# Issue order of the attention weights at the start of a four-block kernel

## The chip, the cores and the metric

The kernel runs on one core of one Trainium2 chip. The metric is device time in microseconds, the median over runs of the whole program. A lower number is better. One further execution was taken with the hardware profiler; its span runs from the first to the last instruction.

## The reference

The program applies four residual blocks to `x` (2048 tokens of width 512, bf16): A, B, A, B, each after a layer norm. Block A is a recurrent attention with a memory of 8 rows: it goes through 64 segments of 32 tokens in order, and the memory rows of one segment's output are the memory of the next. Block B is a linear attention over all tokens at once. Both A blocks use the same weights.

```python
for s in range(n_seg):                       # 64 segments of 32 tokens
    xs = x[:, s * seg_len:(s + 1) * seg_len, :].copy()
    h = jnp.concatenate([mem, xs], axis=1)   # 8 memory rows, 32 tokens
    q = jnp.einsum('btd,dhe->bhte', h, Wq)   # Wq, Wk, Wv: 512 x 32 heads x 128
    k = jnp.einsum('btd,dhe->bhte', h, Wk)
    v = jnp.einsum('btd,dhe->bhte', h, Wv)
    scores = jnp.einsum('bhqe,bhke->bhqk', q, k) * scale
    scores = jnp.where(mask[None, None], scores, -1000000000.0)
    p = _softmax(scores, axis=-1)
    o = jnp.einsum('bhqk,bhke->bhqe', p, v)
    o = jnp.einsum('bhte,hed->btd', o, Wo)   # Wo: 32 heads x 128 x 512
    mem = o[:, :M, :].copy()
    outs.append(o[:, M:, :])

x = x + _A_ref(_layernorm(x, axis=-1), A_mem0, A_Wq, A_Wk, A_Wv, A_Wo, A_seg_len)
x = x + _B_ref(_layernorm(x, axis=-1), B_wqkv, B_wo)
x = x + _A_ref(_layernorm(x, axis=-1), A_mem0, A_Wq, A_Wk, A_Wv, A_Wo, A_seg_len)
x = x + _B_ref(_layernorm(x, axis=-1), B_wqkv, B_wo)
```

## The kernel before

**Weights.** `Wq_sb`, `Wk_sb`, `Wv_sb` and `Wo_sb` hold the four weights of block A in SBUF, 4 MB each, for the whole program. The first three are loaded by one DMA each from ACT's queue (line 651). `Wo_sb` comes in four quarters of 1 MB from SP's queue (line 656). Quarters 0 and 1 carry a dependence on the key load (`late[1]`), quarters 2 and 3 on the value load (`late[2]`). The load of block B's `wqkv` follows on SP (line 658) and depends on the last quarter in program order; POOL's load of block B's output weight (line 663) depends on that one.

**A segment.** `a_layer` goes over the 64 segments. Memory rows and the first 24 tokens of a segment make one block of 32 columns; the last 8 tokens of four segments together make another, the left block of a group of four segments (`left_block`). For each block, `project` (matmul line 785) multiplies with a weight into one PSUM bank, 16 matmuls for one of two halves of the heads, four of them side by side in column tiles. `turned` copies the result to an image in SBUF and transposes it, either on PE (line 807, evacuated through line 619 or 618) or, for later left blocks and some keys, with a DMA transpose from SP's queue (line 798). Images of left blocks take turns in two slots; an image is not overwritten before the DMA transpose that reads it has landed. Then come the scores of the memory rows (line 876), their sums and values (lines 903, 916, 917), the scores within the left block (line 835), attention of the tokens (lines 948, 945, 971, 972), the output projection with `Wo_sb` (line 999), and with line 1024 the memory rows for the next segment. Line 618 is the evacuation of a PSUM bank when ACT does it, line 619 when DVE does it. A few matmuls on unused data (line 735, `warm`) stand in the first segment.

In the first segment the transposes from SP's queue are those of the left block of the second group, which the planner brings forward into the head of the program: four of them, called T1 to T4 here in their order on SP. Line 835 for that group needs all four.

**Order of the work.** The order on every engine is made before the program is emitted. Each operation is added to a list with its engine or engines, a cost, and what it reads and writes. `schedule` then walks a modelled time. Whenever an engine is free it takes, among the operations whose inputs are ready in the model, the one with the highest priority. For an operation with a place the priority is minus its due time, which is its step times `PERIOD` plus an entry of the table `OFFSET`:

```python
        for nd in nodes:
            nd.prio = nd.tail
            if nd.key is not None and OFFSET:
                step, name, k = nd.key
                nd.prio = -(step * PERIOD + OFFSET[name][k])
```

Operations without a place, such as the four quarters of `Wo`, have as priority the length of the longest modelled chain of work behind them. `finalize` turns dependences into semaphore waits: an instruction waits on its engine's in-order queue, and all that stands behind it waits too. PSUM banks are given out in the course of the same planning.

**The loads at the start.** They carry places with large negative steps:

```python
    P.at(-9000, "ld0")
    P.at(-8000, "ld1")
    for i, (W, v, nm, t) in enumerate(((Wq_sb, qk_view[0], "Wq", 13.2), (Wk_sb, qk_view[1], "Wk", 23.7),
                                       (Wv_sb, qk_view[2], "Wv", 34.8))):
        P.at(-9000 + 1000 * i, "ld%d" % (2 + i))
```

`ld0` is the load of the first memory, `ld1` that of the first 128 rows of `x`, both on SP; `ld2`, `ld3` and `ld4` are the loads of Wq, Wk and Wv on ACT. The step of Wv is -7000, but its offset of -27049.20 puts its due time ahead of the others, so ACT issues Wv, Wq, Wk. The last numbers (13.2, 23.7, 34.8) are the modelled landing times, used only for planning.

Of the kernel before, what the change touches and what calls it, by code (L numbers as in the profile page):

```python
# [22 lines left out]

PERIOD = 13.5
OFFSET = {
    "ld0": (-123.05,),
    "ld1": (-42.20,),
    "ld2": (6.75,),
    "ld3": (-61.40,),
    "ld4": (-27049.20,),  # L30
    "startF": (31.55,),
    "prepF": (60.65, -70.40, -52.45, 13.25, -87.60, -51.75, -71.05, 30.70, -58.30, 4.70, -58.20),
    "left0F": (-67.40, -16.05, 42.40, -9.10, 43.45, -14.00, -72.75, 13.95, -5.65, 15.60, -9.65, -120.75, 45.95,
# [1303 lines left out]
```

## Time and profile before

| | |
|---|---|
| median of 3 runs | 1804.88 us (1804.27 to 1810.15) |
| profiled execution | 1801.99 us |
| its span | 1799.8 us, mean granted TensorE clock 0.991 |
| PE busy | 1690.6 us (94%) |
| PE weight loads | 1138.5 us (63%) |
| ACT busy | 1166.0 us (65%) |
| DVE busy | 954.5 us (53%) |
| POOL busy | 325.9 us (18%) |
| PE's first matmul with Wq | 24.43 us after the start of the span |
| PE's first matmul with Wk | 35.94 us |
| PE's first matmuls with Wv | from 49.88 us |
| PE's first matmul with Wo | about 61.1 us |

The busy shares are averages over the span; the head of the program, before the first matmul with `Wo_sb`, is about 61 of the 1800 us and has its own limits. PE is the tensor engine's matmuls and PEld its weight loads, which overlap. SPq and ACTq are the queues of DMA issues on those engines. An idle time labelled "issue" is one for which the profile shows no wait. Rows of one line and shape are merged in the timeline, so a row's length can span pieces of other rows.

### The profile page before, as it was taken

To read this page: it belongs to the slowest core of one execution; us is meant where nothing else is said; L and a number is where in the kernel's file an instruction comes from. 1 tells how busy PE (TensorE), PEld (TensorE's weight loads), DVE (VectorE), ACT (ScalarE), POOL (GpSimd) and SP (SyncE) were. 2 spreads that over 40 slices of the span, in tenths; PEclk is the share of its full clock that TensorE was granted. 3 is DMA by queue.
4 is the path that set the end of the run, shared out by engine and by line. 5 is a ranking of instruction groups with operands and counts; after the bars stand their busy time and mean duration, and the time that the engine had idled before them with its cause. 6 is when DMAs were issued, how large, how long until landed. Compare 5 with 4: busy or idle time off the path is not lost.

```text
span 1799.8 us, 104863 instructions
## 1 busy us (share of the span) xinstructions
PE 1690.6 (94%) x48407; PEld 1138.5 (63%) x48407; DVE 954.5 (53%) x3216; ACT 1166.0 (65%) x3109; POOL 325.9 (18%) x660
## 2 busy tenths in 40 slices
PE   3899999999999999999889999999999999999997
PEld 1566676667666676676556666666666666666673
DVE  2355455555555555555554555555555555545456
ACT  2566666666666666666556666666667677666665
POOL 2012111211211121121101112222111222211220
PEclk9999999999999999999999999999999999999998
DMA  8412222222222222122111222212222222231223
GB/s 341 116 38 41 45 44 47 42 47 42 45 43 42 47 44 45 41 44 46 28 24 33 48 46 45 50 44 45 47 44 51 44 45 48 47 47 40 57 65 110
DMA packets 235080, 99.29 MB, mean 55 GB/s; under 512 B 213624, under 2 KB 228784, under 8 KB 233104
## 3 DMA queue, kind: packets, MB, share of 16 engines
q1 hardware_dynamic: 211312, 60.22, 17.1%
q0 software_dynamic: 21744, 19.78, 4.7%
q10 hardware_dynamic: 1584, 12.58, 1.7%
q8 instruction: 379, 6.21, 1.4%
q14 instruction: 61, 0.50, 0.1%
HBM read 29.63 MB, written 10.49 MB: 22 GB/s over the span
## 4 chain that ended last, share of the span: by engine, by line
PE 75%; DMA 12%; DVE 5%; ACT 3%; issue 2%; POOL 1%; ACTq 0%; DVEq 0%
PE pb L785 38%; PE pb L999 13%; DMA arena_sb<-arena_sb 9%; PE pb L971 3%; PE pb L1161 3%; PE pb L876 3%; PE pb L807 2%; PE pb L903 2%; DMA Wk_sb<-in_A_Wk_dram 2%; PE pb L1195 2%; POOL dx_sb L634 1%; ACT arena_sb L618 1%; DVE arena_sb L619 1%; PE pb L948 1%; PE pb L1024 1%
## 5 line engine op out<-in xcount | busy, mean ns | idle before, releaser
L618 ACT ACTIVATE arena_sb<-pb 128x512 bf16<-128x512 f32 (+5 forms) x1387 | 705.5, 511 | 330.6 <-PE pb L785 275.7
L634 POOL DMA_DIRECT2D dx_sb<-y_sb x504 | 253.2, 509 | 869.5 <-DVE y_sb L1035 491.8
L785 PE MATMUL pb<-Wv_sb,arena_sb 128*32 128x512 bf16 x5120 | 380.2, 380 | 0.0
L619 DVE COPY arena_sb<-pb 128x512 bf16<-128x512 bf16 (+2 forms) x365 | 131.5, 361 | 398.0 <-PE pb L807 382.5
L785 PE MATMUL pb<-Wq_sb,arena_sb 128*32 128x512 bf16 x5120 | 320.7, 381 | 10.2 <-DMA Wq_sb<-in_A_Wq_dram 9.9
L999 PE MATMUL pb<-Wo_sb,arena_sb 128*32 128x256 bf16 x10368 | 317.2, 274 | 7.5 <-DVE arena_sb L920 7.3
L785 PE MATMUL pb<-Wk_sb,arena_sb 128*32 128x512 bf16 x5120 | 320.2, 381 | 3.8 <-DMA Wk_sb<-in_A_Wk_dram 3.3
L999 PEld LDWEIGHTS pb<-Wo_sb,arena_sb 128*32 128x32 bf16 x10368 | 264.5, 97 | 30.7 <-DVE arena_sb L920 17.7
L785 PEld LDWEIGHTS pb<-Wq_sb,arena_sb 128*32 128x32 bf16 x5120 | 141.8, 97 | 132.1 <-DMA Wq_sb<-in_A_Wq_dram 10.2
L785 PEld LDWEIGHTS pb<-Wk_sb,arena_sb 128*32 128x32 bf16 x5120 | 134.7, 97 | 119.7 <-DVE arena_sb L619 11.1
L619 DVE CAST arena_sb<-pb 128x512 bf16<-128x512 f32 (+3 forms) x346 | 165.0, 478 | 70.4 <-PE pb L785 37.6
L619 DVE COPY arena_sb<-arena_sb 32x320 bf16<-32x320 bf16 (+1 forms) x677 | 150.1, 222 | 81.0 <-PE pb L876 62.7
L618 ACT ACTIVATE outW_sb<-pb 128x128 fp32r<-128x128 f32 x323 | 89.6, 277 | 124.4 <-PE pb L999 118.9
L876 PEld LDWEIGHTS pb<-arena_sb 128*32 128x32 bf16 x8128 | 109.5, 94 | 84.5 <-DMA arena_sb<-arena_sb 35.3
L876 PE MATMUL pb<-arena_sb 128*32 128x8 bf16 x8128 | 131.5, 174 | 29.8 <-DMA arena_sb<-arena_sb 24.5
L785 PEld LDWEIGHTS pb<-Wv_sb,arena_sb 128*32 128x32 bf16 x5120 | 121.8, 95 | 55.1 <-issue 1.6
L971 PE MATMUL pb<-arena_sb 128*128 128x128 bf16 x1024 | 145.3, 218 | 1.4 <-issue 0.6
L887 ACT ACTIVATE arena_sb<-pb 128x192 bf16<-128x192 f32 (+1 forms) x256 | 83.8, 328 | 93.7 <-PE pb L876 92.1
L972 PE MATMUL pb<-arena_sb 128*128 128x32 bf16 x1024 | 127.4, 178 | 0.1
L1035 DVE TENSOR_TENSOR y_sb<-pb,outW_sb 64x256 bf16<-64x256 f32 x158 | 65.9, 417 | 97.0 <-ACT outW_sb L618 93.6
L807 PEld LDWEIGHTS pb<-id_sb,arena_sb 128*32 128x32 bf16 x4352 | 84.3, 96 | 44.7 <-issue 8.1
L894 DVE TENSOR_TENSOR arena_sb<-arena_sb 128x128 bf16<-128x128 bf16 x504 | 90.1, 221 | 39.6 <-ACT arena_sb L887 38.7
(116 smaller groups left out, 2139.8 us busy)
## 6 DMA issues: line engine op xcount, KB each, us to landing
arena_sb<-arena_sb SPq DMA_TRANSPOSE x368, 2.8
Wv_sb<-in_A_Wv_dram ACTq DMA_DIRECT2D x1, 4096.0 KB, 13.6
Wq_sb<-in_A_Wq_dram ACTq DMA_DIRECT2D x1, 4096.0 KB, 23.1
Wk_sb<-in_A_Wk_dram ACTq DMA_DIRECT2D x1, 4096.0 KB, 34.1
Wo_sb<-in_A_Wo_dram SPq DMA_DIRECT2D x4, 1024.0 KB, 7.1
xs_scratch<-x_sb POOLq DMA_DIRECT2D x32, 128.0 KB, 2.2
pq_scratch<-arena_sb POOLq DMA_DIRECT2D x32, 128.0 KB, 2.0
dx_sb<-y_sb POOLq DMA_DIRECT2D x252, 12.0 KB, 2.0
```

What stands on the lines that cost most here:

```text
L618: return e.activation(o() if callable(o) else o, i() if callable(i) else i, ACTF.Copy)
L619: return e.tensor_copy(o() if callable(o) else o, i() if callable(i) else i)
L634: add(eng, lambda e: e.dma_start(o, i), 0.55 if eng == "pool" else 0.4, reads=reads, writes=writes, dsem="%s%d" % (kind, k), lat=lat + (0. ...
L785: r = pe.matmul(tl.f32()[32 * j:32 * j + 32, 0:512], blk[:, c, :], W[:, c, o:o + 512], start=(c == 0), stop=(c == 3), tile_position=(0, 32 ...
L807: r = pe.transpose(tt.bf16()[32 * j:32 * j + 32, 128 * i:128 * i + 128], img[:, k, o:o + 32], id_sb[:, :], tile_position=(0, 32 * j))
L876: r = pe.matmul(tl.f32()[32 * j:32 * j + 32, 48 * i + o:48 * i + o + n], kk[:, hh, j, :], qT[:, hh, j, 0:n], start=True, stop=True, tile_p ...
L887: add("act", lambda a: a.activation(PQ[:, r2, b, :, 0:nq], tl.f32()[:, 0:192].rearrange("p (i q) -> p i q", i=4)[:, :, 0:nq], ACTF.Exp, sc ...
L894: add("dve", lambda v, a=a: v.tensor_tensor(Pm[:, k, a, :].rearrange("p (i j x) -> p i j x", i=4, j=4), PQ[:, r2, b, :, 40 * a:40 * a + 8] ...
L971: pe.matmul(o, vimg[:, r2, e], Pbx[:, hh, :, 0:32], start=True, stop=False)
L972: return pe.matmul(o[:, :, 24:32], vleft[:, g2, e], Pbx[:, hh, :, 32:40], start=False, stop=True)
L999: r = pe.matmul(tl.f32()[32 * j:32 * j + 32, 0:256], oT[:, 4 * hh + n, :], Wo_sb[:, 8 * n + hh, 256 * d:256 * d + 256], start=(hh == 0 and ...
L1035: add("dve", lambda v: v.tensor_tensor(y_sb[0:64, k, :], tl.f32()[0:64, 0:256], outW[64:128, w, :].bitcast(F32), ALU.add), c_dve(256), rea ...
```

## The change

Five entries of `OFFSET` become zero. With them the due times are -121500 for the first memory and for Wq, -108000 for the first rows of `x` and for Wk, and -94500 for Wv.

```diff
--- before.py
+++ after.py
@@ -23,11 +23,11 @@
 
 PERIOD = 13.5
 OFFSET = {
-    "ld0": (-123.05,),
-    "ld1": (-42.20,),
-    "ld2": (6.75,),
-    "ld3": (-61.40,),
-    "ld4": (-27049.20,),
+    "ld0": (0.00,),
+    "ld1": (0.00,),
+    "ld2": (0.00,),
+    "ld3": (0.00,),
+    "ld4": (0.00,),
     "startF": (31.55,),
     "prepF": (60.65, -70.40, -52.45, 13.25, -87.60, -51.75, -71.05, 30.70, -58.30, 4.70, -58.20),
```

ACT then issues Wq, Wk, Wv. The planner runs again from these due times, so that the order of some work in the first segment moves too. On PE, with shapes as the emitted program has them (- before, + after; "x16" is sixteen matmuls; the rows shown are those around the first key matmuls and the last value matmuls ahead of `Wo`):

```diff
-L785 Matmult pb<-Wq_sb,arena_sb 32x512 x12
+L785 Matmult pb<-Wq_sb,arena_sb 32x512 x16
 L715 Matmult pb<-arena_sb 128x128
 L785 Matmult pb<-Wq_sb,arena_sb 32x512 x4
-L785 Matmult pb<-Wk_sb,arena_sb 32x512 x48
+L785 Matmult pb<-Wk_sb,arena_sb 32x512 x4
+L785 Matmult pb<-Wq_sb,arena_sb 32x512 x4
+L785 Matmult pb<-Wk_sb,arena_sb 32x512 x8
+L785 Matmult pb<-Wq_sb,arena_sb 32x512 x8
+L785 Matmult pb<-Wk_sb,arena_sb 32x512 x36
...
-L785 Matmult pb<-Wq_sb,arena_sb 32x512 x16
...
+L785 Matmult pb<-Wv_sb,arena_sb 32x512 x12
 L971 Matmult pb<-arena_sb 128x128
 L972 Matmult pb<-arena_sb 128x4x8
...
+L785 Matmult pb<-Wv_sb,arena_sb 32x512 x4
 L835 Matmult pb<-arena_sb 32x32 x32
-L785 Matmult pb<-Wv_sb,arena_sb 32x512 x16
 L999 Matmult pb<-Wo_sb,arena_sb 32x256 x64
```

On ACT, the evacuation that waits for the landing of T1 (the second query image of the left block) now stands ahead of the first key images; the evacuation of the mask block goes from ACT to DVE. The order on SP and POOL is the same as before.

## The prediction

> **What bounds the kernel now.** I read the table of DMA issues first, since the edit moves DMA issues. Its columns are destination and source, queue, count, size, and us from issue to landing.
>
> ```profile
> Wv_sb<-in_A_Wv_dram ACTq DMA_DIRECT2D x1, 4096.0 KB, 13.6
> Wq_sb<-in_A_Wq_dram ACTq DMA_DIRECT2D x1, 4096.0 KB, 23.1
> Wk_sb<-in_A_Wk_dram ACTq DMA_DIRECT2D x1, 4096.0 KB, 34.1
> Wo_sb<-in_A_Wo_dram SPq DMA_DIRECT2D x4, 1024.0 KB, 7.1
> ```
>
> Three equal loads go out within 1.5 us and land about 10 us apart, one after another: values, queries, keys. The timeline of the first 64 us (start, length, engine, line, operands, idle time before and its releaser) says who needs them when.
>
> ```profile
> 24.43 4.25 PE L785 MATMUL pb<-Wq_sb,arena_sb 128*32 128x512 bf16 x40 [9.90 <-DMA Wq_sb<-in_A_Wq_dram]
> 33.35 1.30 SPq L798 DMA_TRANSPOSE arena_sb<-arena_sb  x1
> 35.92 1.02 SPq L656 DMA_DIRECT2D Wo_sb<-in_A_Wo_dram  x2
> 35.94 4.05 PE L785 MATMUL pb<-Wk_sb,arena_sb 128*32 128x512 bf16 x48 [3.26 <-DMA Wk_sb<-in_A_Wk_dram]
> ...
> 43.35 5.16 SPq L798 DMA_TRANSPOSE arena_sb<-arena_sb  x2
> 45.85 0.25 PE L835 MATMUL pb<-arena_sb 128*32 128x32 bf16 x11 [2.27 <-issue]
> 48.55 1.21 SPq L656 DMA_DIRECT2D Wo_sb<-in_A_Wo_dram  x2
> ...
> 49.88 0.10 PEld L785 LDWEIGHTS pb<-Wv_sb,arena_sb 128*32 128x32 bf16 x3
> 53.16 1.19 SPq L798 DMA_TRANSPOSE arena_sb<-arena_sb  x1
> 59.10 0.30 PE L835 MATMUL pb<-arena_sb 128*32 128x32 bf16 x16 [1.84 <-DMA arena_sb<-arena_sb]
> 59.22 1.89 PE L785 MATMUL pb<-Wv_sb,arena_sb 128*32 128x512 bf16 x16
> 60.88 2.70 PE L999 MATMUL pb<-Wo_sb,arena_sb 128*32 128x256 bf16 x64
> ```
>
> PE waits 9.90 us for Wq and 3.26 us for Wk, while Wv, landed at 14.4, is first read at 49.88. The chain of waits over the first 90 us agrees: its two long DMA pieces are
>
> ```profile
> 1.83 34.07 DMA Wk_sb<-in_A_Wk_dram
> ...
> 53.16 5.80 DMA arena_sb<-arena_sb
> ```
>
> The second is the fourth transpose, queued behind the last two Wo quarters. From 64.8 us PE runs from segment to segment, and no wait there names a weight load. So the head is DMA-bound, and what it ends earlier the whole kernel ends earlier.
>
> Last, the DMA view of 6 to 8 us, where ACT's loads (q10, 8 KB packets) meet an x load on SP's queue (q1, 1 KB) and POOL's (q0):
>
> ```profile
> q10 hardware_dynamic: 70, 0.57, 69.2%
> q0 software_dynamic: 64, 0.20, 24.7%
> q1 hardware_dynamic: 72, 0.07, 10.3%
> ```
>
> 72 packets against 70: the queues take turns packet by packet, not byte by byte.
>
> **What the Trainium skill says.** "DMA: Bandwidth & Descriptors", Queues, rings and completion order: each engine goes round its queues in turn, and descriptors of one queue are consumed in ring order. The packet counts above agree, and so does the fourth transpose, which needs 5.8 us behind Wo where a free queue takes 2.5. "Runtime: NRT & Kernel Launch", Instruction fetch mechanics: instructions come in 16 KiB blocks over a DMA queue of their own. The trace has such a fetch at 43.26 to 44.34 us, and PE, idle for "issue" since 43.6, goes on at 45.85. "TensorE: Matmul & The Clock Gate", What's actually happening: a free-running window of about 3.4 us decides between half and full clock. Here the clock is half from 35.16 to 38.57 and from 59.05 to 62.47, 3.41 us each, after idle stretches.
>
> **The change, part by part.** Five start offsets become zero. Two of them are no change of order: x and memory inputs stay first on SP. ACT's three issues become Wq, Wk, Wv. SP's order is unchanged: transpose T1; Wo quarters 1 and 0 (waiting for Wk); T2, T3; quarters 3 and 2 (waiting for Wv); T4; wqkv. What is new is when those waits end. Wk lands second, Wv last, so the first two quarters now start while Wv is still moving. On PE the same matmuls are reordered within the first segment; from the second segment on, order and waits are the same on every engine but for a few waits already met, with PSUM banks renamed.
>
> 1. *Queries.* The first load now feeds PE. It lands at 0.80 + 13.6 = 14.4, so PE starts at 14.45 instead of 24.43: 9.98 us gained. Its inputs are ready: the first group's evacuations end by 13.1, the rest at 15.96, when PE is still in its first cold groups (0.43 us for four matmuls, so the first evacuation came 2.8 us after the start).
> 2. *Keys.* Query work took 24.43 to 32.7, so it ends near 22.7. The second load lands at 24.4. The old third one was late by some 1.5 us on one DMA engine (15 of its 16 completions by 34.3, the last at 35.90, after an instruction fetch and T1). Those meet Wk again at the same distance, so I take 25.9: 10.0 us earlier, with the PE idle as long as before.
> 3. *The 2.27 us instruction stall* stays: its fetch again falls among weight traffic. Shifted, PE goes on at 35.9; up to 1 us later if two loads delay the fetch more than one.
> 4. *Values.* Old third landing 34.3 without the fetch. Added: T1 in the middle of the stream, about 1 us (its data took 34.6 to 35.9); Wo's packets one for one with some 370 remaining packets of Wv, 46 against 309 ns, so 7.4 us become 8.5, +1.1; a fetch on one engine, +1.1. That is 37.5. PE asks at 49.88 - 10.0 = 39.9. Hidden, with 2.4 us to spare; without that cover each us is a us.
> 5. *SP's queue, the next thing late.* By Wv's end Wo has moved 370 KB of its first 2048. The rest at the 355 KB/us of 40 to 43 us takes 4.7 us: 41.8. T2 and T3, waiting behind it, 1.1 us each: 44.0. Quarters 3 and 2, 2048 KB at about 345: 50.0. T4: 51.0, landed 51.3. Before, 58.97; so T4 gains only 7.7 of the 10. ACT's evacuation for T4's image waits for T3, which lands near 44.3, not 42.5; the attention work behind it on ACT moves 1.8 us, and PE would reach the L835 pair near 49.7. So T4 still decides.
> 6. *After T4.* Before, PE then ran L835 (0.30), 16 Wv matmuls (1.71, cold) and L999 at 61.11. Now the Wv matmuls stand ahead of L835: L999 starts at 51.3 + 0.14 + 0.30 = 51.75. That is 9.36 us earlier. L999 took 2.5 us with part of it cold; all warm it is 1.77 (the next segment's), all cold 3.5. I charge 0.3.
>
> Sum: 9.36 - 0.3 = 9.1 us. The span goes from 1799.8 to 1790.7, the profiled execution from 1801.99 to 1792.9. The median of the runs, 1804.88, is 2.9 above that execution; taken from it the time is 1795.8.
>
> Moved but free: the mask-block evacuation goes from ACT to DVE, which idles there; wqkv waits for quarter 3 and then T4, lands near 55 instead of 62.9, and is first needed when block B starts, tens of us later.
>
> **Unknowns, bounded.** T1 now flows against a full stream of 8 KB packets; the trace shows it only against the tail of one. If its 32 rows on each engine go as a burst, as T2's and T3's do alone, it costs about 1 us and lands near 26.5 to 28; PE's next query image needs it at 28.5. If each row of 256 bytes takes turns with an 8 KB packet, 32 x 0.33 = 10.6 us, so it lands at 35. I take the burst: POOL's 1 KB packets that meet a transpose later in the trace are held for 1 us and more, not the transpose. Clock: the phase of the half-rate stretches may cost or give 1.7 us. Both ends are kept in the range.
>
> **Rivals.**
>
> *T1 crawls behind Wv.* ACT's in-order queue has the second query image (it waits for T1) ahead of the key images. With T1 landed at 35, ACT stands from about 28 on, PE soon after, and the key images come out at 36.1 to 38.5 instead of 39.2 to 41.8: only 3.3 to 3.6 us are gained, 1801.4. For it: strict turns in the lines above. Against it: the held POOL packets.
>
> *The queue costs less than I say.* If Wo moves faster or T4 slips in early, PE is the limit: it comes to L835 at 47.9, L999 at about 48.8, saving 12: 1793.
>
> *Wv becomes the bound.* The wait only changes its name from Wk to Wv. If the queues shared by bytes, Wv would land near 41, and PE would wait 1 us, still less than T4 costs. It would have to land after 44 to erase more than 3 us; this only widens the forecast.
>
> *Slower.* The renamed PSUM banks stay renamed through all 128 segments. If a clash of banks cost each segment 0.15 us, 19 us would be lost, 10 more than gained: 1814.8. It decides above 0.07 us a segment, and would be measurably slower above 0.115. Nothing in the trace names a bank as a reason for waiting, and every wait is on the same producers as before.
>
> **How the numbers follow.** Likeliest 0.68: 1795.8, own range 1793.3 to 1798.3. Queue faster 0.08: 1793. T1 crawls, or some mixture of late T1, T3 and fetch, 0.17: 1801.4. Banks 0.07: 1814.8. About 0.3%, 5.4 us, is what a measurement here can tell from no change. Faster: 0.68 + 0.08 = 0.76; same 0.17; slower 0.07. Range 1792.5 to 1801.8: it leaves out the bank case, the far edge of the crawl, and a little below.
>
> **What would show it.** Right: PE's first query group near 14.5, key group near 25.9, no wait for Wv, T1 landed before 28.5, T4 near 51 and L999 near 51.8, then the same length to the end as before. Wrong: a long ACT wait for a transpose near 28; PE waiting for Wv; T4 landed after 54; or a span from L999 to the end that grew.

## The result and the profile after

The changed kernel takes 1804.45 us (median of 4 runs, 1802.95 to 1808.35) where the kernel before took 1805.18 us beside it (4 runs, 1804.27 to 1810.15). The ratio is 0.9994, 95% interval 0.9969 to 1.0018: no difference. The forecast was 1795.8 us, and its range ended at 1801.8. A later comparison with more runs (22 against 59) gives 0.998, interval 0.9968 to 0.9992, so 1.4 to 5.8 us of a forecast of 9.

Executions of one kernel spread over 8 to 15 us here (the kernel before: 1801.88 to 1816.36 in those 59). Where a step of 1 to 5 us in the head of the program is in question, I therefore go by the traces, of which there are two for each kernel.

| us from the start of the span | before | before, again | after | after, again | forecast |
|---|---|---|---|---|---|
| PE's first matmul with Wq | 24.43 | 24.28 | 14.45 | 14.57 | 14.45 |
| PE's first matmul with Wk | 35.94 | 35.64 | 25.88 | 25.54 | 25.9 |
| Wv landed | 14.45 | 14.29 | 37.16 | 36.80 | 37.5 |
| T1 landed | 36.38 | 36.54 | 37.37 | 37.00 | 26.5 to 28 |
| T2, T3 landed | 45.87, 49.79 | 45.84, 49.32 | 43.73, 47.48 | 43.39, 47.03 | by 44.0 |
| T4 landed | 58.97 | 58.84 | 56.61 | 56.26 | 51.3 |
| first line-1024 group (end of the head) | 63.96 | 62.25 | 59.34 | 59.12 | none given |
| second line-1024 group (end of segment 1) | 75.13 | 74.24 | 73.62 | 74.08 | none given |
| span | 1799.8 | 1802.2 | 1803.3 | 1802.7 | 1790.7 |

The loads came as foreseen. The table of DMA issues of the changed kernel:

```profile
Wq_sb<-in_A_Wq_dram ACTq DMA_DIRECT2D x1, 4096.0 KB, 13.6
Wk_sb<-in_A_Wk_dram ACTq DMA_DIRECT2D x1, 4096.0 KB, 24.6
Wv_sb<-in_A_Wv_dram ACTq DMA_DIRECT2D x1, 4096.0 KB, 35.3
Wo_sb<-in_A_Wo_dram SPq DMA_DIRECT2D x4, 1024.0 KB, 11.8
```

The three places are taken by Wq, Wk, Wv, about 11 us apart. Wo's quarters now take 11.8 us instead of 7.1, because two of them, issued at 25.85 and 26.29, stand behind T1 in SP's ring: Wo's first packet moved at 33.78. The timeline of the head of the changed kernel (start, length, engine, line, operands, idle time before and its releaser):

```profile
14.45 3.95 PE L785 MATMUL pb<-Wq_sb,arena_sb 128*32 128x512 bf16 x40
22.80 1.33 SPq L798 DMA_TRANSPOSE arena_sb<-arena_sb  x1
25.85 7.18 SPq L656 DMA_DIRECT2D Wo_sb<-in_A_Wo_dram  x2
25.88 0.62 PE L785 MATMUL pb<-Wk_sb,arena_sb 128*32 128x512 bf16 x4 [3.26 <-DMA Wk_sb<-in_A_Wk_dram]
37.46 1.57 ACT L618 ACTIVATE arena_sb<-pb 128x512 bf16<-128x512 f32 x3 [14.68 <-DMA arena_sb<-arena_sb]
38.08 8.11 SPq L798 DMA_TRANSPOSE arena_sb<-arena_sb  x2
38.59 0.62 PE L807 MATMUL pb<-id_sb,arena_sb 128*32 128x128 bf16 x16 [6.59 <-ACT arena_sb L618]
47.93 1.69 PE L785 MATMUL pb<-Wv_sb,arena_sb 128*32 128x512 bf16 x28
51.16 1.19 SPq L798 DMA_TRANSPOSE arena_sb<-arena_sb  x1
56.74 0.28 PE L835 MATMUL pb<-arena_sb 128*32 128x32 bf16 x16 [0.67 <-DMA arena_sb<-arena_sb]
57.03 1.93 PE L999 MATMUL pb<-Wo_sb,arena_sb 128*32 128x256 bf16 x64
```

The 9.90 us of waiting for Wq are gone, and a new wait has come: ACT stands idle for 14.68 us, and a transpose ends it. It is the evacuation of the second query image of the left block, which may not overwrite its slot before T1 has landed. PE had finished its matmuls by 28.6, so nearly 9 us of it are due to T1. Behind it in ACT's queue are the evacuations of the key images, so PE, done with the key matmuls, stands with it, 6.59 us by the profile. The pieces of over 5 us made of transposes in the chain of waits say the same:

```profile
22.80 14.57 DMA arena_sb<-arena_sb
...
51.16 5.44 DMA arena_sb<-arena_sb
...
61.94 5.18 DMA arena_sb<-arena_sb
```

The first is T1 and the second T4. The third is new too: two key transposes of segment 1, which took about 2.9 us in the kernel before (issued 66.56, landed 69.42). The head is 4.62 us shorter than before, and segment 1 gives 3.11 of it back (63.96 to 75.13 took 11.17 us before; 59.34 to 73.62 takes 14.28). In the second pair of traces the head wins 3.13 us, and 2.97 are given back (11.99 us of segment 1 against 14.96).

Last, the DMA view of 29 to 31 us: q10 carries Wv in packets of 8 KB, q1 carries T1 in rows of 256 bytes. The columns are packets, MB, and their share of 16 engines.

```profile
q10 hardware_dynamic: 100, 0.82, 97.7%
q1 hardware_dynamic: 98, 0.03, 5.5%
```

98 rows go against 100 packets: one for one. T1's 512 rows, 32 for each of the 16 engines, start from 26.8 to 36.6 us. In the kernel before they did so from 34.6 to 35.9. Taking turns is not all of these 9.9 us. By 33.5 us 315 rows had moved. Then Wv ran out (23 packets in the half us before, 10 and 2 in the two after), and 109 rows moved in half a us. The last row moved at 36.63, 0.4 us after Wv's last packet (36.24). So T1 kept pace with Wv's packets while these lasted, and landed when the last straggling ones were over.

### The profile page after: what moved, and what is told of

It is laid out like the page before. It is cut to its first block, busy times and chain, and to the rows that moved or that the text cites. A ratio compares the mean times of both kernels' runs of the same rounds, so it can differ in the third digit from the quotient of the medians.

```text
span 1803.3 us, 104862 instructions
## 1 busy us (share of the span) xinstructions
PE 1692.2 (94%) x48407; PEld 1140.7 (63%) x48407; DVE 954.7 (53%) x3217; ACT 1165.2 (65%) x3108; POOL 325.9 (18%) x660
## 4 chain that ended last, share of the span: by engine, by line
PE 73%; DMA 14%; DVE 6%; ACT 3%; issue 2%; POOL 2%; DVEq 0%; SPq 0%; ACTq 0%
PE pb L785 37%; PE pb L999 13%; DMA arena_sb<-arena_sb 12%; PE pb L971 3%; PE pb L1161 3%; PE pb L876 3%; PE pb L807 2%; PE pb L903 2%; POOL dx_sb L634 2%; PE pb L1195 1%; DVE arena_sb L619 1%; DMA dx_sb<-y_sb 1%; ACT arena_sb L618 1%; PE pb L948 1%; PE pb L917 1%
## 5 line engine op out<-in xcount | busy, mean ns | idle before, releaser
L999 PE MATMUL pb<-Wo_sb,arena_sb 128*32 128x256 bf16 x10368 | 316.7, 273 | 7.5 <-DVE arena_sb L920 6.7
L999 PEld LDWEIGHTS pb<-Wo_sb,arena_sb 128*32 128x32 bf16 x10368 | 263.8, 97 | 30.3 <-DVE arena_sb L920 17.3
L785 PEld LDWEIGHTS pb<-Wv_sb,arena_sb 128*32 128x32 bf16 x5120 | 121.5, 95 | 55.3 <-issue 1.0
L807 PE MATMUL pb<-id_sb,arena_sb 128*32 128x128 bf16 x4352 | 109.1, 220 | 7.6 <-ACT arena_sb L618 7.1
## 6 DMA issues: line engine op xcount, KB each, us to landing
Wo_sb<-in_A_Wo_dram SPq DMA_DIRECT2D x4, 1024.0 KB, 11.8
```

Of the source, the lines that this page charges most:

```text
L785: r = pe.matmul(tl.f32()[32 * j:32 * j + 32, 0:512], blk[:, c, :], W[:, c, o:o + 512], start=(c == 0), stop=(c == 3), tile_position=(0, 32 ...
L807: r = pe.transpose(tt.bf16()[32 * j:32 * j + 32, 128 * i:128 * i + 128], img[:, k, o:o + 32], id_sb[:, :], tile_position=(0, 32 * j))
L999: r = pe.matmul(tl.f32()[32 * j:32 * j + 32, 0:256], oT[:, 4 * hh + n, :], Wo_sb[:, 8 * n + hh, 256 * d:256 * d + 256], start=(hh == 0 and ...
```

## The experiments

Two theories were to be told apart at first. **A**: T1 crawls behind Wv, and the evacuation that waits for its slot at the head of ACT's queue takes the gain. **B**: the sheer traffic of Wv and Wo makes everything late. In all diffs below, which are shortened, "-" is the changed kernel. A head or a second group that is some us "ahead" is measured from the first trace of before; from its second trace it is 1.71 us less in the head and 0.89 us less at the second group.

### T1 to T4 from images of their own

```diff
-            nd = evac(img[:, k, :], ...)
+            nd = evac(own_img[n], ...)        # n = 0..3, buffers that are free at this time
```

> The changed kernel, but the four transposes T1 to T4 read images in buffers of their own, so no evacuation waits for a transpose to land; SP's order becomes T1, T2, two Wo quarters, T3, T4, two Wo quarters. Theory A (T1 crawls behind Wv, and ACT's in-order queue stands behind the image slot that T1 holds): T1 still lands near 37 us, but ACT doesn't stand; the first key images come near 28.5 instead of 38, PE has no 6.6 us wait for ACT, the first matmul with Wo moves from 57.0 to 51 to 53, and the first memory step (L1024) from 59.3 to 53 to 55. Theory B (the head is bound by the sheer traffic of Wv and Wo, the wait for the slot only covers it): PE waits for Wv or Wo instead, and Wo starts not before 56.

1801.23 us (one run; before on the same chip 1804.72, median of 23). T1 again crawled (48 rows against 48 packets of 8 KB in each us from 25 to 31, landed at 36.15), and now nothing on ACT waited for it; the key matmuls, transposes and scores ran from 25.7 to 35.7. But with these images the planner put T2 ahead of Wo and T3 and T4 between its quarters, and its PE order asks for them earlier. The timeline:

```profile
46.48 0.48 PE L844 MATMUL pb<-arena_sb 128*32 128x32 bf16 x32 [7.10 <-DMA arena_sb<-arena_sb]
```

PE waited 7.10 us for T3 and T4, and a stretch of half clock (44.70 to 51.53) lay over the end of this wait and what followed. The first matmul with Wo came at 55.76, not at 51 to 53, so the head was only 5.90 us ahead. Theory A is right on T1 and ACT; the first matmul with Wo is nearly as late as theory B had it. The slot wait can be taken away and the gain is still held up: the ring of SP's queue, with Wo ahead of the transposes, is the second thing in the way.

### Wv in eight pieces with packets of 1 KB

```diff
-        a.dma_start(W[:, :, :], v)
+        for f in range(8): a.dma_start(W[:, :, 512*f:512*f+512], v[:, :, 512*f:512*f+512])
```

> The changed kernel, but Wv is loaded in eight pieces of 512 columns, so in packets of 1 KB instead of 8 KB; SP now has T2, T3, T4 ahead of the last two Wo quarters. Theory A (one row of T1 per packet of Wv, so the pace is set by the packet's length): with 46 ns instead of 309 ns a turn T1 lands at 28 to 30 us instead of 37. Theory B (T1 is slow because the DMA engines are full, whatever the packets): T1 still lands at 35 or later. Side effect expected under A: Wo takes half of the turns from Wv, so Wv lands near 42 and PE waits for it by some 2 us; Wo's first matmul near 53.

1812.53 us (one run), 8 us slower than before, and it says nothing on T1. The timeline of its start:

```profile
1.83 27.41 ACTq L656 DMA_DIRECT2D Wv_sb<-in_A_Wv_dram  x8
29.28 1.28 ACT L675 ACT_TABLE_LOAD   x1 [29.28 <-issue]
```

Eight issues held ACT until 29.2 us, so all that ACT does for the layer norm began there and PE's first query group came at 34.27. Wv was in at 36.39, so that T1, issued at 42.70, met none of it.

### Wv on SP's queue, behind T1

```diff
-        a.dma_start(W...)   on ACT, third
+        sp.dma_start(W...)  on SP, after T1
```

> The changed kernel, but Wv is issued on SP, right behind T1, so both share one queue and T1's rows come first. Theory A: T1 lands by 27.5 us, ACT doesn't stand, Wv lands near 37, Wo's first matmul near 51 and the first L1024 near 53 (59.3 in the changed kernel): 6 us gained in the head. Theory B: Wo's first matmul not before 56. In time: the head's gain less what the first segments give back; 1797 to 1802 under A.

(So that this wait could be added, the planner works out the chain lengths in the order of the dependences, here and in the two runs that hold a load back.) 1799.74 us (median of 20), ratio to before 0.9971 (0.9960 to 0.9983): the time that was expected, but not by the way expected. T1 landed at 26.57, so without Wv in its way it takes 3.9 us from its issue. The timeline then shows what is late next:

```profile
38.59 0.83 PE L799 MATMUL pb<-Wv_sb,arena_sb 128*32 128x512 bf16 x12 [2.51 <-DMA Wv_sb<-in_A_Wv_dram]
...
54.03 0.30 PE L851 MATMUL pb<-arena_sb 128*32 128x32 bf16 x16 [4.57 <-DMA arena_sb<-arena_sb]
```

PE waited 2.51 us for Wv, which landed at 38.55. The last transpose landed at 53.90 behind the last Wo quarters (52.75), and Wo as a whole began later, since it now follows Wv in one ring (its first packet moved at 35.95, in the changed kernel at 33.78). A stretch of half clock (51.44 to 58.27) lay over the matmuls with Wo. The first line-1024 group came at 59.37, as in the changed kernel; L999 near 51 was missed. What it has over the changed kernel is that segment 1 gave nothing back (second group at 70.54, 4.6 us ahead of before).

### All four transposes on PE

```diff
-        turned(Wq_sb, ..., False, step > 0)      # transpose by DMA
+        turned(Wq_sb, ..., False, step > 0 and not on_pe)   # PE, line 807, in the first segment
```

> The changed kernel, but the four transposes of the second group's left block are done on PE (4 x 16 matmuls of some 0.2 us a group, four DVE evacuations of 0.42 us), so SP carries only Wo in the head. Theory A: key images near 28.5, Wv lands near 36.5 without being waited for, Wo's first matmul near 49.5 and the first L1024 near 51.5, 8 us before the changed kernel's. Theory B: not before 56. In time 1795 to 1801 under A.

1793.01 us (median of 4), ratio 0.9939 (0.9918 to 0.9959): faster than both kernels, and than expected. The timeline:

```profile
47.56 1.93 PE L1004 MATMUL pb<-Wo_sb,arena_sb 128*32 128x256 bf16 x64 [0.51 <-issue]
...
58.24 0.28 PE L881 MATMUL pb<-arena_sb 128*32 128x40 bf16 x16 [2.23 <-DMA arena_sb<-arena_sb]
```

The head ends at 49.87, 14.09 us ahead of before; 64 more transposes on PE cost less than PE's waits. Against the changed kernel's head (4.62 ahead) the four transposes in SP's queue cost 9.5 us. Segment 1 gave 4.8 back: its two key transposes, the first issued at 52.47, met POOL's load of block B's output weight (its data moved from 53.3 to 55.3, theirs from 55), and an instruction fetch at 56.37; a stretch of half clock (58.49 to 65.32) followed the wait.

### The changed kernel again

> The changed kernel once more, timed in more rounds and with a second trace. Theory A: the head gains 4.6 us (first line-1024 group near 59.3 us) and the first following segment gives 3.1 back, so the time is 0.5 to 3 us below before, about 1803.2; the trace again shows T1 landing near 37 us and segment 1's key transposes near 67. Theory C (the give-back is chance and the head's 4.6 us normally last): 1800.

1805.21 us (median of 22) against 1807.06 (59): the ratio 0.998 (0.9968 to 0.9992) given above. As theory A said, T1 landed at 37.00, ACT waited 14.51 us for it, the head was 4.84 us ahead of the first trace of before, and segment 1's key transposes landed at 66.90, 5.2 us after their issue; PE waited 1.68 us for them. The time alone does not decide between the two theories: its interval, 1.4 to 5.8 us below before, holds what either says.

### Block B's output weight held back to segment 2

```diff
+    wob.sync.add(<the last operation of mem1 in segment 2>)   # POOL's load waits for it
```

> The changed kernel with POOL's load of block B's output weight held back until segment 2. Theory A: the 3.1 us that segment 1 gives back come from this load meeting segment 1's two key transposes; without it they land within 3 us of their issue (near 64.9 us instead of 66.9), PE has no wait of 1.5 us for them, the second line-1024 group keeps 4 to 4.6 us on before, and the time is about 3 us below the changed kernel: 1799 to 1801. Theory B (the give-back comes with the half-rate clock stretch or with another wait in segment 1): the second line-1024 group stays 1.5 us ahead of before and the time is as of the changed kernel, 1803.

1804.10 us (median of 22), ratio to before 0.9986 (0.9974 to 0.9997). In the trace the mechanism is there. The wait for the key transposes in segment 1, first in the changed kernel, then with the load held back:

```profile
67.17 0.28 PE L876 MATMUL pb<-arena_sb 128*32 128x40 bf16 x16 [1.53 <-DMA arena_sb<-arena_sb]
```

```profile
66.74 0.28 PE L886 MATMUL pb<-arena_sb 128*32 128x40 bf16 x16 [0.33 <-DMA arena_sb<-arena_sb]
```

Fifteen of the 16 completions of the first key transpose came by 65.14, 2.45 us after its issue (5.2 in the changed kernel); the last came at 66.70, after an instruction fetch (64.6 to 65.6). Segment 1 gave back 0.7 us instead of 3.1. About half of the difference is the wait; in this trace no half-rate stretch lay over the segment either, where the changed kernel had one from 68.95 to 72.37 (its 64 matmuls with Wo took 2.91 us there, 1.92 here). The total time, however, is not 3 us below the changed kernel's: the medians differ by 1.1 us, and the ratios to before (0.9986 here, 0.998 there) not even in that direction. All fourteen traces bear out the meeting. Where the load's data were over or held back, that transpose took 2.4 to 2.5 us from its issue (four traces, leaving out the one late completion here); where they were still moving, it took 2.9 to 5.7. PE's wait for it was 1.3 to 2.2 us in the four with more than 4.5 us, and 0 to 0.7 elsewhere. In each of these four a stretch of half clock also lay over segment 1, and of the other ten over one (over another for its first 0.2 us), so wait and clock come together and their shares are not told apart. So that the load meets the transposes is shown; what it costs in the whole time is not.

### The old load order, with the four transposes on PE

> The old order of the loads (Wv, Wq, Wk), with the four transposes of the second group's left block on PE. It asks what the order of the loads is worth once no transpose stands in SP's queue. Theory A: the old order then waits for Wk at 35.9 us and its own work after that, so the first matmul with Wo comes at 57.5 to 59.5 us and the time is 1.5 to 4 us below before, 1801 to 1803; the order of the loads is then worth about 10 us of the 11.7 that the new order showed with PE transposes. Rival D: the transposes alone were the bound and the load order is worth little: time 1793 to 1796.

The edit is that of "All four transposes on PE", applied to the kernel before. 1800.35 us (median of 20), ratio 0.9965 (0.9952 to 0.9978), 6.3 us below before. The head ended at 57.94, 8.1 us later than with the new order of the loads (49.87), and the times lie 4.7 us apart (6.3 against 11.0 below their own runs of before). Neither expectation was met: the first matmul with Wo came at 55.64, before the 57.5 that theory A had, so the transposes alone are worth more than it said, and the time is not as low as rival D said. Once they are off SP's queue the order of the loads is worth 8.1 us in the head, most of what the forecast promised, and about half of it in the time.

### The transposes on PE, and the output weight held back

> The new order of the loads, the four transposes on PE, and block B's output weight held back until segment 2. Theory A: head 14 us ahead of before as in the run with PE transposes, and the 4.9 us that its segment 1 gave back are kept: second line-1024 group 13 to 14 us ahead, time 1788 to 1791. Theory B: as with PE transposes alone, 1793.

1792.93 us (median of 6), ratio 0.9917 (0.9891 to 0.9942): the lowest here, though its interval overlaps that without the second edit. The head was 10.97 us ahead and not 14, because PE stood in the middle of the matmuls with Wo:

```profile
48.20 1.69 PE L1014 MATMUL pb<-Wo_sb,arena_sb 128*32 128x256 bf16 x53
...
52.11 0.51 PE L1014 MATMUL pb<-Wo_sb,arena_sb 128*32 128x256 bf16 x11 [2.22 <-issue]
```

Nothing that the profile shows was awaited there; an instruction fetch ran from 49.81 to 50.83. Segment 1's first key transpose landed 2.5 us after its issue, with no wait, and the second line-1024 group came at 65.85, as without the edit (65.88). The edit is not shown to be worth anything here.

### T1 alone on PE

```diff
-        turned(Wq_sb, ..., False, step > 0)
+        turned(Wq_sb, ..., False, step > 0 and not (first half of the heads, in the first segment))
```

> The changed kernel with T1 alone done on PE; the other three transposes stay in SP's queue, at the places that they had among the Wo quarters or one place earlier. No evacuation at the head of ACT's queue then waits for a transpose that meets Wv. Theory A (the late T1 is the step that failed): ACT has no wait near 28 us, PE runs its key images near 28 to 31, the last transpose lands at 51 to 52.5, the first line-1024 group comes 8 to 10 us ahead of before instead of 4.6, and the time is 5.5 to 8 us below before. Theory E (Wo's quarters in SP's ring hold the last transposes whatever T1 does): last transpose at 54 or later, first line-1024 group at most 6 us ahead, time 2 to 4.5 us below before, as of the changed kernel.

The head follows theory A. The timeline:

```profile
25.62 2.77 PE L786 MATMUL pb<-Wk_sb,arena_sb 128*32 128x512 bf16 x48 [1.40 <-DMA Wk_sb<-in_A_Wk_dram]
...
52.13 0.30 PE L837 MATMUL pb<-arena_sb 128*32 128x32 bf16 x16 [1.36 <-DMA arena_sb<-arena_sb]
52.42 3.44 PE L1001 MATMUL pb<-Wo_sb,arena_sb 128*32 128x256 bf16 x64
```

ACT had no wait for a transpose; the key images followed from 27.59. The second query image's transpose, now first on SP, crawled in T1's place (landed 36.54) with nobody waiting. The last transpose landed at 52.08 (expected 51 to 52.5). The matmuls with Wo lay in half clock (45.32 to 55.56) and took 3.44 us, so the first line-1024 group came at 56.24, 7.72 us ahead (8 to 10 expected). But the time was 1804.01 us (median of 14), ratio 0.9987 (0.9973 to 1.0002), about 2 us below before, not 5.5 to 8.

### The same a second time

> The kernel with T1 alone on PE a second time, because its head came 7.7 us ahead but its time only 2.4 us below before. If the rest of the 1700 us differed by chance: head again 7 to 9 us ahead, and the time now 4 to 8 us below before. If something later in this program takes back what the head wins: head again 7 to 9 us ahead, and the time again 1 to 3 us below before.

1807.21 us (median of 14), ratio 1.0004 (0.9990 to 1.0019). The head was 7.80 us ahead, the second group 7.5. So the head's gain repeats, and in the time it is again not there: something later in this program takes it back. In both traces it goes in the same segments, mostly of the second pass of block A. Counted from 0, and against the median of all fourteen traces, segments 63 to 124 took 11.0 and 13.3 us longer here; 0.0 and 1.7 longer in the two traces of before; 5.1 and 0.2 in those of the changed kernel. Segment 70 of the second trace:

```profile
1016.70 0.28 PE L878 MATMUL pb<-arena_sb 128*32 128x40 bf16 x16 [1.76 <-DMA arena_sb<-arena_sb]
```

Fifteen completions of the key transpose came by 1014.81 and the 16th at 1016.65, with an instruction fetch from 1014.3 to 1015.6. In the first trace of the same program the same segment had the 15th at 1020.84, the 16th at 1022.43, and the fetch from 1020.4 to 1021.3. In the two traces each of before and of the changed kernel all 16 of that transpose landed within 0.2 us, in three of them 0.4 us ahead of the fetch, in one just as it began. Segment 122 shows the same pattern. Two segments are not 11 us: that the fetches account for all of it is not shown.

### Wv in two loads with packets of 4 KB

```diff
-        a.dma_start(W[:, :, :], v)
+        a.dma_start(W[:, :, 0:2048], v[:, :, 0:2048])
+        a.dma_start(W[:, :, 2048:4096], v[:, :, 2048:4096])
```

> The changed kernel with Wv loaded by two DMAs of packets of 4 KB instead of one of 8 KB; nothing else moves. Theory A (T1's rows take turns one for one with Wv's packets, so the size of these sets its pace): 32 rows against 4 KB packets need about half as long, so T1 lands at 31 to 33 us instead of 37, ACT's wait for it falls from 14.7 to about 9 us, and Wv itself lands unchanged near 37. Theory B (T1 waits for the traffic of Wv to end): T1 again lands with Wv at 37.

1800.66 us (one run; before 1806.38). The pace is as theory A says. The DMA view of 29 to 31 us, as above:

```profile
q10 hardware_dynamic: 188, 0.76, 94.5%
q1 hardware_dynamic: 176, 0.05, 10.6%
```

With packets of half the size, 176 rows pass in 2 us instead of 98, again about one for one. Yet T1 landed at 36.56, not at 31 to 33: the second load's issue held ACT's queue until 11.06, so that the layer norm and with it all of PE's work came some 2 us later, and T1 was issued at 25.03. Its first row moved 3.9 us after that, as in the changed kernel, and an instruction fetch at 31.13 stopped both streams for more than a us. From its first row to its last took 6.7 us instead of 9.9. ACT's idle time fell to 11.64 us, not to 9. Here the last row (35.60) moved before Wv's last packet (37.08). So theory A is shown for the pace, while the landing was missed.

### The kernel before again

> The kernel before, traced once more. If the drift of up to 5 us between segment 24 and the end, seen between the first traces of the two kernels, is chance of the execution, two traces of this one kernel differ as much over that stretch; the head agrees within 0.5 us. If the drift came from the change, they agree within 1 us everywhere.

1804.35 us in one run. Its head ended at 62.25 instead of 63.96: the half-rate stretch that lay over the matmuls with Wo in the first trace (59.05 to 62.47) fell elsewhere (36.69 to 40.10). So the head did not agree within 0.5 us. Over the segments that follow, the two traces of one program part by 3.3 us (1.71 ahead at the first group, 1.6 behind at the 33rd). From segment 24 to the end, where the question was put, they part by some 2 us, neither within 1 nor by up to 5. So a drift of 2 to 3 us between two traces need not be an effect of a change; whether one of 5 is, stays open.

## Why the prediction was wrong

**Queries and keys (steps 1, 2)** were right to 0.1 us: 14.45 and 25.88.

**Instruction stall (step 3)** did not stay. The fetch came at 33.03 to 34.04, when PE stood waiting for ACT anyway, and line 835 went on at 43.45 with no stall. It was a forecast of a phase that the rest of the step undid.

**Values (step 4)** were right in the number: Wv landed at 37.16 (37.5 forecast), and PE first read it at 47.93. That is partly luck. The 1.1 us charged for Wo's packets was not there, since only 20 of them had moved by 34.0. In their place, none of Wv's 16 completions came before 36.88, just after T1's last row; with all transposes on PE 14 of them came by 35.02 and the last at 36.62.

**T1, under "Unknowns, bounded": the step that failed in the head.** The bound from below was T1 as a burst (landing 26.5 to 28), the bound from above a row against each 8 KB packet (10.6 us, landing at 35), and I took the burst. The measured movement is 9.9 us (26.8 to 36.6), close to the bound from above. Even that bound put the landing 2.4 us too early, because the first row moved only 4.0 us after T1's issue, where the trace of before had 1.3 (33.35 to 34.63). The strict turns of the bound are what the counts show, but that its 10.6 us come so near is partly luck, since T1 ended with Wv and not after 32 turns. In five traces (the changed kernel twice, with the output weight held back, and T1 on PE twice, where the second query image's transpose stands in T1's place) the rows of SP's first transpose took 7.0 to 9.9 us, and its last row moved 0.4 to 0.5 us after Wv's last packet each time. With images of their own T1 began at 22.35 and needed all its turns: 12.6 us, two stops of up to about a us included. My reason for the burst was that POOL's 1 KB packets were held when they met a transpose. That was another pair of queues, not this one, and half a reading: at 452.5 us of that trace rows of a transpose are held 1.6 to 1.7 us beside POOL's packets, held 1.6 to 1.8. The 72 packets against 70 shown for 6 to 8 us, on the other hand, were of the very queues concerned. "DMA: Bandwidth & Descriptors" of the Trainium skill, Queues, rings and completion order, says that an engine drains a whole packet of typically 9 to 17 descriptors from one ring before it turns to the next. That would have let a transpose's rows through in groups; the records here, one row to one 8 KB packet, do not look so, and the measurement decides.

**SP's queue (step 5)** followed from that. T2 could be issued only at 38.08, once ACT had written its image, and T3, whose image needs the key matmuls on PE, at 45.00. T3 landed at 47.48 (44.0 forecast), the last quarters of Wo, issued behind it, at 55.97 (50.0), T4 at 56.61 (51.3). So 3.5 of T4's 5.3 us stand at T3 already. A term of this step was also too small: the last quarters landed 8.5 us after T3, as in the kernel before (49.79 to 58.33), where I had 6.0. With T1 on PE, T4 landed at 52.08: the outcome of this step was right to 0.8 us once T1 is out of the way, with the last quarters at 51.53, 7.2 us after the transpose ahead of them. The runs with Wv behind T1 and with images of their own show that T1 is not the only guard: as long as transposes stand behind Wo's quarters in one ring, a later one can take its place.

**After T4 (step 6).** The matmuls with Wo began at 57.03 instead of 51.75, 5.28 us late, and ran warm in 1.93 us; the head's gain was 4.62 us.

**"Moved but free"** failed as well. wqkv landed at 60.5, not near 55, and I asked only when it is needed. Behind it stands POOL's load of block B's output weight. It was issued at 60.79, its data moved from 62.3 to 64.6, and they met segment 1's key transposes (issued 61.94, landed 67.1); in the first trace of the kernel before the load had landed at 67.4 and their rows began at 67.7. The four traces in which PE waited 1.3 us or more for this gave back 3 to 5 us in segment 1, measured from the first trace of before; the others gave back 0 to 1.7. The half clock that lay over segment 1 in these four is part of it.

**From the head to the end: the second step that failed.** "What it ends earlier the whole kernel ends earlier" fits the four transposes on PE (9.2 us ahead after segment 1, 11.0 below in the time) and Wv behind T1 (4.6 and 5.2), but not T1 alone on PE (6.9 and 7.5 ahead in its two traces; 2.4 and nothing in the time). There T1 is out of the way and T4 lands nearly as forecast, and still the time is missed. So T1 explains what the head lost, not all that is missing in the time, and why that program loses its gain later stays open. For the changed kernel, the 9.1 us of the forecast were 4.6 and 3.1 in the head of the two pairs of traces, 1.5 and 0.2 after segment 1, and 0.7 and 1.9 by the medians of the two comparisons. Where the rest of the second comparison's interval (1.4 to 5.8 us) would come from, the traces do not show.

**The rivals.** "T1 crawls behind Wv" was the right one: its ACT wait from about 28 us came as described, and its gain of 3.3 to 3.6 us was 3.1 and 4.6 in the heads of the two pairs of traces. Its time, 1801.4, was not met in the first comparison; the interval of the second holds such a gain. It had 17 in 100, since I let a resemblance outweigh a count. The renamed PSUM banks are not shown to cost anything: the rest after segment 1 takes 2.9 us longer in the mean of two traces (1729.2 against 1726.3), less than the two traces of before differ (3.2). That would be 0.02 us a segment, where the rival supposed 0.15.

## What to carry to other kernels

When a load order changes, list for every DMA that is issued while the new stream runs what waits for its landing, and whether that wait sits at the head of an in-order queue: here 128 KB of transposed rows held ACT and then PE. Where two bounds of an unknown lie 8 us apart, look for the row of the trace that has the same queues and the same kind of packets, count, and ask when the other stream ends. And a head that ends earlier moves all that follows against the loads and instruction fetches still under way, so check the first segment after it too, and trace the kernel before twice before reading a difference of 1 to 3 us.

## What the hardware did that I had not expected

- A DMA transpose's rows of 256 bytes took turns with the load's packets one for one at both sizes that were tried: 98 against 100 of 8 KB in 2 us, 176 against 188 of 4 KB. While the load lasts, the size of its packets sets the transpose's pace.
- Under a full stream the first row moved 3.9 to 4.0 us after the issue, instead of 1.3.
- Beside some instruction fetches (about 1 us each, 379 in the 1803 us of the changed kernel) one of a transpose's 16 completions came 1.6 to 1.8 us after the 15th, and in the two traces of one program this fell in the same segments, 70 and 122. "Runtime: NRT & Kernel Launch" of the Trainium skill, Instruction fetch mechanics, calls the cost of crossing a block mostly hidden; here waits beside single ones were 1.8 to 2.3 us long (PE stalls of 2.27 us in the kernel before and of 2.22 with the transposes on PE and the output weight held back, and 1.76 through a transpose).
- A DMA issue can hold its engine's queue for long behind other loads: behind Wq and Wk, eight issues of 512 KB in packets of 1 KB held ACT until 29.2 us, and the second of two issues of 2 MB in packets of 4 KB until 11.06. One of 4 MB in packets of 8 KB did not hold it. What decides is not shown.
